# Soft MoE behind attention on one core: a group's shifts, its combine steps, the experts' loads and the borrowed parts in another order

## The chip, the cores and the metric

The kernel runs on one core of a Trainium2 chip. The metric is the device time of one execution in microseconds. It was run three times before the change; the median counts.

## The reference

Attention without softmax runs over 8 batches of 2496 tokens; its output, 19968 rows of 256, goes through a soft mixture of 8 experts with 4 slots each. Cut to what matters:

```python
scores = (z @ z.transpose(0, 2, 1)) / S        # z: 8 x 2496 x 64
x = u * (np.maximum(scores, 0.0) ** 2 @ v)     # u, v: 8 x 2496 x 256
x = x.reshape(B * S, D)
logits = x @ phi                               # 19968 x 32
d = np.exp(logits - logits.max(0)); d /= d.sum(0) + 1e-09
slot_input = d.T @ x                           # 32 slots
# each expert: h = np.maximum(slot_input[e] @ w1[e], 0.0); slot_out[e] = h @ w2[e]
c = np.exp(logits - logits.max(1, keepdims=True)); c /= c.sum(1, keepdims=True) + 1e-09
out = c @ slot_out
```

## The kernel before

**Half steps.** The attention is cut into half steps, 50 for each of batches 0 to 6 (numbers 0 to 349) and 60 for the last (350 to 409). A half step takes two tiles of 128 keys against a chunk of up to 512 queries; ten of them in a row (their place is `at`, 0 to 9) make a chunk of x. The main loop (line 1001) handles half step h: it calls `transfers(h)` (line 905, DMAs that come due), then `weights(last)` (experts' loads by the number of half steps that are left, `W_LOADS`, line 854, from 58 before the end on), then one item of the list `work` if `at` is at least 2 or 20 or fewer are left, and then TensorE's sums of half step h, with `prepare` (line 428) of half step h+3 in their midst, h+2 in the first ones.

**What `prepare(k)` does.** TensorE writes the scores of k (line 352) to `sc`, the only tile of the pool `sc_ps` (line 90). ScalarE reads it with a relu to `r` and squares `r`. The values are then split in two 16-bit parts: the high part `ph` is a cast by ScalarE or VectorE, the low part `pl` is VectorE's difference `r` minus `ph`; TensorE sums `ph` and `pl` times v into `acc`. Since the scores are symmetric, parts are reused: VectorE transposes `r` to `y` (a half step that turns) and SyncE stores it (`turned`), so that a later half step fetches its `r` and needs no scores (a turned half step; ScalarE only casts). A half step whose keys are its own queries takes half of its values so: one half step transposes to `yd` and lends them (`lent`, line 487), the next fetches them as `rd` (`borrow`, line 497) and does scores for the other half only (128x2x256 for the relu). `transfers` calls `borrow(k)` up to 5 half steps ahead of k (line 917).

**Two lists.** What `work` puts into `middle` is run on ScalarE between the relu and the square of the next `prepare` (for a turned half step ahead of its cast); what it puts into `behind` is run at the end of it, on VectorE.

**Groups.** The rows of x are taken in groups of 1024 (0 to 19), and `groups(q)` (line 626) makes the list of 15 items that `work` then hands out one per half step, so over two chunks, eight for each (`todo`, line 778, for groups 0 to 17). Its items: `logits` (products of x and phi, copied to `L` by VectorE); `ex` (the dispatch exponential `E`, into `middle`); four `blocks` and `e` (transposes of x and of E to `y`, behind); four `shifts` (each issues four DMAs of a quarter from `y` to `xt`, so that slots and tokens lie for the slot sums); `c0` (`combine`: transpose of `L` in place, its maximum `rm`, the difference, all on VectorE); `c1` (`combine_exp`: exponential of `L` on ScalarE, into `middle`); `c2` (`combine_sum`: sum, add, reciprocal and product); `c3` (the transpose to `cw`) together with an entry for the slot sums in `late`. The slot sums of group q (line 708) run on TensorE within `logits` of group q+1 and read `xt`.

**Order.** Each engine works in the order in which the program is written (`InOrder`). SyncE issues every DMA, in one queue. All engine calls go through one helper, so the trace gives line 74 for them and the tiles tell them apart.

Of the kernel before, what the change touches and what calls it, by code (L numbers as in the profile page):

```python
# [77 lines left out]
def attn_soft_moe_kernel(ctx, tc, uT, v, zz, phi, ww, outT):  # L78
# [37 lines left out]
    def take_blocks(b):  # L116


        for j in BLOCKS[b == B - 1]:
            zt[b, j] = blk.tile([P, 2, 512], F16, tag="blk", name=f"z_{b}_{j}")  # L120
        for i in range(2 * NP):
            vt_[b, i] = blk.tile([P, 2, 2, D], F16, tag="blk", name=f"v_{b}_{i}")
# [202 lines left out]
    pend, arriving, scratch, staged = {}, {}, {}, {}  # L325
# [5 lines left out]
    def run(todo):  # L331
        now, todo[:] = todo[:], []
        for f in now:
            f()

    def fetch(k):

        x = halves[k]
        j, o, n, _ = x.ch
        if n < PAD + PAD:  # L340
            r = wa.tile([P, 2, 4, P], F32, tag="r", name=f"r_{k}", bufs=4)
        else:
            r = turns_sb.tile([P, 4, 4, P], F32, tag="y", name=f"r_{k}")
        a0, na = o // P, r.shape[1]
        sp.dma_start(
            r.rearrange("p a j r -> p a (j r)"), scratch[x.b, x.p, j][:, a0 : a0 + na]
        )
        for i in range(2):
            w = halves[k + i].w
            arriving[k + i] = r[:, :, 2 * w : 2 * w + 2].rearrange("p a h r -> p h a r")  # L350
# [146 lines left out]
    def borrow(k):  # L497

        x = halves[k]
        r = turns_sb.tile([P, 4, 2, 2 * NS], F32, tag="rd", name=f"rd_{k}", bufs=1)  # L500
        sp.dma_start(r.rearrange("p a j r -> p a (j r)"), scratch.pop((x.b, x.p, x.p)))
        arriving[k] = r.rearrange("p a j r -> p j a r")
# [117 lines left out]
    def shift(src, a):  # L620


        for b in range(4):
            sp.dma_start(xt[32 * b : 32 * b + 32, a], src[32 * a : 32 * a + 32, b])

    def groups(q):
# [6 lines left out]
        def own(tag, *shape):  # L633
            if tag not in tiles:
                tiles[tag] = wk.tile([P, *shape], F32, tag=tag, name=f"{tag}_{q}", bufs=1)
            return tiles[tag]

        L, E, y = lambda: own("L", 2 * P), lambda: own("E", 2 * P), lambda: own("y", 4, NB)
# [36 lines left out]
        def turn_block(j, c):  # L675
            dve.transpose(
                y()[:, :, j * D : (j + 1) * D].rearrange("p b (t c f) -> p c t b f", t=4, c=2)[:, c],
                x[:, c, 512 * j : 512 * (j + 1)].rearrange("p (t b k) -> p t b k", t=4, b=4),
            )
# [50 lines left out]
        def turn_x_whole(i):  # L730
            j, t0 = i // 2, i % 2 * 2
            ps = ms_ps.tile([P, 2, 512], F32, tag="ms", name=f"xt_{q}_{i}")
            for k in range(2):
                turn_x(ps[:, k], x, 4 * j + t0 + k)
            for k in range(2):
                copy_x(act.copy, ps[:, k, 0:D], xt[:, t0 + k, j * D : (j + 1) * D])
# [34 lines left out]
        blocks = [lambda j=j, c=c: behind.append(lambda: turn_block(j, c)) for j in range(2) for c in range(2)]  # L771
        shifts = [lambda a=a: shift(y(), a) for a in range(4)]
        e, c0, c2, c3 = (lambda f=f: behind.append(f) for f in (turn_e, combine, combine_sum, combine_turn))
        ex, c1 = (lambda f=f: middle.append(f) for f in (exps, combine_exp))
        rest = lambda: None
        if q < NQG - 2:

            todo = [logits, ex, *blocks, e, shifts[0], c0, shifts[1], c1, shifts[2], c2, shifts[3]]
            todo.append(lambda: (c3(), late.append(slot_sums)))
        else:  # L780


            todo = [rest, rest, logits, ex, lambda: behind.append(adding.pop(0)), lambda: behind.append(add_counts)]
            todo += [c0, c1, c2, c3, turn_e_whole, *[lambda i=i: turn_x_whole(i) for i in range(4)]]
            todo.append(lambda: late.append(last_slot_sums))
# [36 lines left out]
    def load_w(i):  # L822
        t = w_raw[i]
        if isinstance(t, list):
            for k in range(2):
                sp.dma_start(t[k], ww[i][:, k * 512 : (k + 1) * 512])
        else:
            sp.dma_start(t, ww[i].rearrange("p (k n) -> p k n", k=2))
# [31 lines left out]
    def weights(left):  # L860

        if left in W_TAKES:
            W_TAKES[left]()
        for i in W_LOADS.get(left, ()):
            load_w(i)


    def load_u(b, ch):
        _, _, n, t0 = ch
        ut = wa.tile([P, 2, QC], F32, tag="ut", name=f"ut_{t0}", bufs=1)  # L870
        q0 = t0 - b * S
        sp.dma_start(
            ut[:, :, :n], uT[b, :, q0 : q0 + n].rearrange("(c p) q -> p c q", p=P)
        )
        ut_[t0] = ut
# [21 lines left out]
    landing, fetched = {}, set()  # L897
    accs = []

    def next_acc():  # L900

        accs.append(acc_ps.tile([P, 2, QC], F32, tag="acc", name=f"acc_{len(accs)}"))
        return accs[-1]

    def transfers(h):

        x = halves[h]
        if x.at == 2:
            load_u(x.b, x.ch)
        for k in range(h + 1, min(h + 9, len(halves))):  # L910
            y = halves[k]

            if y.turned and y.opens and k not in arriving and k not in fetched:
                if k - h <= 7 and (y.b, y.p, y.ch[0]) in scratch:
                    fetched.add(k)
                    fetch(k)
            if y.borrows and k - h <= 5 and k not in fetched and (y.b, y.p, y.p) in scratch:
                fetched.add(k)
                borrow(k)
        for f, b, i, at in splits.get(h + 2, ()):  # L920
            if (b, 0) not in vt_:
                take_blocks(b)
            for step, g in zip(at, f(b, i), strict=True):
                landing.setdefault(step, []).append(g)
        if h in later:
            landing.setdefault(h, []).append(later[h])
        while stores and stores[0][0] <= h + 1:
            stores.pop(0)[1]()

    def split_first_v():  # L930
        if v_splits:
            for f in v_splits.pop(0):
                f()
# [3 lines left out]
    def between_last(k):  # L937

        if k:
            if k == 1:  # L940
                xps.append(sc_ps.tile([P, 2, QC], F32, tag="sc", name="tr_first"))
                two = [raws.tile([P, 2, D], F32, tag="raw", name=f"xt_last_{i}", bufs=NRAW) for i in range(2)]
                xt_last.extend(t[:, i] for t in two for i in range(2))
            ps = xps[0][:, k - 1, 0:D]
            turn_x(ps, xg_[NQG - 1], k - 1)
            copy_x(act.copy, ps, xt_last[k - 1])
# [54 lines left out]
    for h, x in enumerate(halves):  # L1001
        if x.begins:
            chunk = h // (2 * NP)
            acc = accs[chunk] if chunk < len(accs) else next_acc()
        last = len(halves) - h
        transfers(h)
        weights(last)
        if work and (x.at > 1 or last <= 20):
            work.pop(0)()
        behind.extend(landing.pop(h, ()))  # L1010
        ahead = [k for k in range(h + 2 + (h > CATCH), h + 3 + (h >= CATCH)) if k < len(halves) and k >= 3]
        split_first_v()
        if not ahead and h < 1:
            run(middle)
            run(turning)
            run(behind)
            sums_halves(h, acc, 1, sums_halves(h, acc, 0, None))
        elif ahead and not halves[ahead[0]].turned:
            turn = sums_halves(h, acc, 0, None)
            prepare(ahead.pop(0))  # L1020
            sums_halves(h, acc, 1, turn)
        else:
            if ahead and not x.ends:
                prepare(ahead.pop(0))
            elif not ahead:
                run(middle)
                run(behind)
                between_last(3 - last)
            sums_whole(h, acc)
        if x.ends:  # L1030
            finish_chunk(x.b, x.ch, acc)
        for k in ahead:
            prepare(k)
        if h in FIRST_Z:
            z_splits.pop(FIRST_Z[h])()
        del pend[h]
# [300 lines left out]
```

## Time and profile before

| | us |
|---|---|
| runs | 1304.5, 1305.19, 1307.16 |
| median | 1305.19 |
| span of the profiled execution | 1303.9 |
| TensorE (PE) busy | 1259.8 |
| VectorE (DVE) busy | 1100.0 |
| ScalarE (ACT) busy | 933.8 |

The profiled execution has no time of its own beside the span; the median of the runs is 1.3 us above it. In the rows further down a line gives an engine, the operation, the tile that it writes and those that it reads; brackets give idle time of the engine ahead of the instruction and what ended it. A semaphore wait is put down to the event that came last by the profile. The granted clock is TensorE's, 1.00 being 2.4 GHz and 0.50 being 1.2 GHz.

### The profile page before, as it was taken

The page shows a single profiled execution, that of the slowest core. Times are in us where ns is not written, and L with a number is a line of the kernel's source. Part 1 is how long each engine was busy: PE and PEld are TensorE (multiplying, and loading weights), DVE is VectorE, ACT ScalarE, POOL GpSimd, SP SyncE. Part 2 cuts the span into 40 slices and gives each one's busy share as a digit, 9 for nine tenths or more (in the row PEclk, how much of TensorE's full clock was granted, in tenths as well). Part 3 has the DMA queues.
Part 4 walks back from the last instruction along what each step waited for, and adds up shares of the span by engine and source line. Part 5 has one row for each costly group of instructions (what it writes and reads, how often), then busy time and mean ns, then how long its engine had stood idle before and what let it go on. Part 6 is the DMA issues. An engine that isn't in the chain of part 4 may idle for free.

```text
span 1303.9 us, 27620 instructions
## 1 busy us (share of the span) xinstructions
PE 1259.8 (97%) x10961; PEld 609.2 (47%) x10961; DVE 1100.0 (84%) x1587; ACT 933.8 (72%) x1217; POOL 3.7 (0%) x22
## 2 busy tenths in 40 slices
PE   7999999999999999999999999999999999899984
PEld 3444454444544444444544444444544444345752
DVE  6888898789998899789998899789998799766663
ACT  6878697686857788586958688486977778554553
POOL 0000000000000000000000000000000000000000
PEclk7999999999999999999999999999999999999985
DMA  4868758793788757894788757886688858979769
GB/s 138 230 186 263 237 123 241 245 285 120 195 281 269 251 125 224 259 274 152 175 265 274 239 144 211 258 280 192 147 246 267 250 161 229 283 208 321 290 251 379
DMA packets 136402, 298.88 MB, mean 229 GB/s; under 512 B 17872, under 2 KB 38864, under 8 KB 124240
## 3 DMA queue, kind: packets, MB, share of 16 engines
q1 hardware_dynamic: 136272, 297.11, 74.4%
q8 instruction: 86, 1.41, 0.4%
q14 instruction: 44, 0.36, 0.1%
HBM read 162.04 MB, written 113.77 MB: 212 GB/s over the span
## 4 chain that ended last, share of the span: by engine, by line
PE 80%; ACT 7%; DMA 5%; DVE 3%; SPq 2%; issue 2%; ACTq 0%; DVEq 0%; POOLq 0%
PE acc L74 64%; PE sc L74 10%; ACT r L74 4%; PE lg L74 3%; SPq L74 2%; PE pf L74 2%; DMA w_own<-in_w 1%; DMA xt<-y 1%; DVE pl L74 1%; ACT ph L74 1%; ACT ot L74 1%; ACT v L74 1%; DVE y L74 1%; DMA rd<-lent 1%; DMA turned<-y 1%
## 5 line engine op out<-in xcount | busy, mean ns | idle before, releaser
L74 PE MATMUL acc<-ph,v 64*128 64x512 f16 (+5 forms) x5036 | 932.1, 370 | 3.1 <-DVE ph L74 2.0
L74 PEld LDWEIGHTS <-v 64*128 64x128 f16 (+1 forms) x7554 | 470.5, 95 | 527.9 <-issue 40.3
L74 PE MATMUL acc<-pl,v 64*128 64x512 f16 (+5 forms) x2518 | 603.1, 369 | 1.5 <-DVE pl L74 1.2
L74 DVE TENSOR_TENSOR pl<-r,ph 128x1024 f16<-128x1024 f32 (+1 forms) x410 | 466.5, 1146 | 109.6 <-ACT ph L74 98.1
L74 ACT CAST ph<-r 128x1024 f16<-128x1024 f32 (+1 forms) x286 | 288.6, 1018 | 134.3 <-DMA r<-turned 73.2
L74 ACT ACTIVATE r<-sc 128x1024 f32<-128x1024 f32 (+1 forms) x242 | 229.1, 947 | 126.2 <-PE sc L74 124.1
L74 ACT ACTIVATE r<-r 128x1024 f32<-128x1024 f32 (+1 forms) x241 | 237.4, 985 | 6.9
L74 DVE STREAM_TRANSPOSE y<-r 128x1024 f32<-128x1024 f32 x160 | 198.0, 1237 | 0.0
L74 PE MATMUL sc<-z,z 64*128 64x512 f16 x912 | 124.5, 377 | 2.7 <-ACT r L74 2.5
L74 PEld LDWEIGHTS <-z 64*128 64x128 f16 x1380 | 71.1, 94 | 76.5 <-issue 7.6
L74 DVE CAST ph<-r 128x1024 f16<-128x1024 f32 (+1 forms) x124 | 74.1, 598 | 12.9 <-ACT r L74 12.7
L74 DVE SCALAR_TENSOR_TENSOR xg<-acc,out_by,ut 128x1024 f32<-128x1024 f32 (+7 forms) x57 | 51.7, 930 | 10.1 <-PE acc L74 10.1
L74 DVE SCALAR_TENSOR_TENSOR v<-vr,v_by,v 128x512 f16<-128x512 f32 x80 | 57.9, 724 | 0.1
L74 ACT ACTIVATE v<-vr,v_by 128x512 f16<-128x512 f32 x80 | 57.0, 715 | 0.5 <-DVE v_by L74 0.5
L74 ACT ACTIVATE vq<-vr 128x512 bf16<-128x512 f32 x79 | 49.2, 623 | 9.8 <-DMA vr<-in_v 9.5
L74 PE MATMUL sc<-z 64*128 64x512 f16 (+1 forms) x468 | 50.6, 321 | 0.0
L74 DVE STREAM_TRANSPOSE y<-xg 128x512 f32<-128x512 f32 x72 | 49.4, 686 | 0.0
L74 DVE COPY ot<-pf 128x1024 f32<-128x1024 f32 (+1 forms) x20 | 24.0, 1198 | 20.7 <-PE pf L74 20.7
L74 ACT COPY ot<-pf 128x1024 f32<-128x1024 f32 (+1 forms) x20 | 19.8, 991 | 24.4 <-PE pf L74 21.5
L74 ACT CAST ph<-rd 128x512 f16<-128x512 f32 x36 | 21.8, 605 | 18.6 <-DMA rd<-lent 18.6
L74 DVE TENSOR_TENSOR pl<-rd,ph 128x512 f16<-128x512 f32 x36 | 24.0, 666 | 13.0 <-ACT ph L74 12.9
L74 PE MATMUL lg<-xt 64*32 64x256 f32 x576 | 23.7, 392 | 8.5 <-DMA w_raw<-in_w 5.0
(187 smaller groups left out, 540.2 us busy)
## 6 DMA issues: line engine op xcount, KB each, us to landing
turned<-y SPq DMA_DIRECT2D x320, 256.0 KB, 4.9
r<-turned SPq DMA_DIRECT2D x76, 1024.0 KB, 6.4
xt<-y SPq DMA_DIRECT2D x288, 72.0 KB, 3.6
vr<-in_v SPq DMA_DIRECT2D x80, 256.0 KB, 5.4
outT<-ot SPq DMA_DIRECT2D x18, 1024.0 KB, 7.0
ut<-in_uT SPq DMA_DIRECT2D x31, 512.0 KB, 6.2
lent<-yd SPq DMA_DIRECT2D x144, 64.0 KB, 2.9
rd<-lent SPq DMA_DIRECT2D x36, 256.0 KB, 4.3
```

The lines of the kernel that those rows point to most:

```text
L74: return lambda *a, **k: self.tc.keep_in_program_order(f(*a, **k))
```

## The change

In a group's list all four shifts now follow `e` (in which the transposed exponentials are put behind), and `c0`, `c1` and `c2` come after them in three half steps in a row; they had a shift between each two. An experts' load is issued behind the item of `work`, not ahead of it. A borrowed part may be fetched six half steps ahead, not five.

```diff
-            todo = [logits, ex, *blocks, e, shifts[0], c0, shifts[1], c1, shifts[2], c2, shifts[3]]
+            todo = [logits, ex, *blocks, e, *shifts, c0, c1, c2]
             todo.append(lambda: (c3(), late.append(slot_sums)))
...
-            if y.borrows and k - h <= 5 and k not in fetched and (y.b, y.p, y.p) in scratch:
+            if y.borrows and k - h <= 6 and k not in fetched and (y.b, y.p, y.p) in scratch:
...
         transfers(h)
-        weights(last)
         if work and (x.at > 1 or last <= 20):
             work.pop(0)()
+        weights(last)
```

In the rows of the order that follow, a name ends in the number of a half step or group and a running number of the program: `r_57_2355` is `r` of half step 57, `L_1_1885` is `L` of group 1.

ScalarE around half steps 57 to 60, before:

```order
L74 ACTIVATE L_1_1885<-L_1_1885 128x256
L74 ACTIVATE r_57_2355<-r_57_2355 128x1024
L74 CAST ph_57_2366<-r_57_2355 128x1024
L74 ACTIVATE r_58_2406<-sc_58_2407 128x1024
L74 ACTIVATE r_58_2406<-r_58_2406 128x1024
L74 CAST ph_58_2416<-r_58_2406 128x1024
L74 ACTIVATE r_59_2446<-sc_59_2447 128x2x256
L74 ACTIVATE r_59_2446<-r_59_2446 128x2x256
L74 CAST ph_59_2456<-rd_59_2340 128x8x64
L74 ACTIVATE r_60_2515<-sc_60_2516 128x1024
```

And after the change:

```order
L74 ACTIVATE r_58_2406<-sc_58_2407 128x1024
L74 ACTIVATE r_58_2406<-r_58_2406 128x1024
L74 CAST ph_58_2416<-r_58_2406 128x1024
L74 ACTIVATE r_59_2449<-sc_59_2450 128x2x256
L74 ACTIVATE L_1_1885<-L_1_1885 128x256
L74 ACTIVATE r_59_2449<-r_59_2449 128x2x256
L74 CAST ph_59_2460<-rd_59_2292 128x8x64
L74 ACTIVATE r_60_2511<-sc_60_2512 128x1024
L74 ACTIVATE r_60_2511<-r_60_2511 128x1024
```

The exponential of `L` of group 1 moved from between relu and square of half step 57 to between those of half step 59.

VectorE at the same place, before, with the three steps of `c0` on `L_1` behind the first transpose:

```order
L74 STREAM_TRANSPOSE y_55_2274<-r_55_2260 128x2x16x32
L74 STREAM_TRANSPOSE L_1_1885<-L_1_1885 128x256
L74 TENSOR_REDUCE rm_1_1800<-L_1_1885 128x8
L74 TENSOR_TENSOR L_1_1885<-L_1_1885,rm_1_1800 128x256
L74 CAST ph_56_2323<-r_56_2313 128x1024
L74 TENSOR_TENSOR pl_56_2324<-r_56_2313,ph_56_2323 128x1024
L74 STREAM_TRANSPOSE y_55_2274<-r_56_2313 128x2x16x32
L74 TENSOR_TENSOR pl_57_2367<-r_57_2355,ph_57_2366 128x1024
L74 STREAM_TRANSPOSE y_57_2370<-r_57_2355 128x2x16x32
```

And after the change:

```order
L74 TENSOR_TENSOR pl_58_2417<-r_58_2406,ph_58_2416 128x1024
L74 STREAM_TRANSPOSE y_57_2374<-r_58_2406 128x2x16x32
L74 STREAM_TRANSPOSE L_1_1885<-L_1_1885 128x256
L74 TENSOR_REDUCE rm_1_1800<-L_1_1885 128x8
L74 TENSOR_TENSOR L_1_1885<-L_1_1885,rm_1_1800 128x256
L74 TENSOR_TENSOR pl_59_2461<-rd_59_2292,ph_59_2460 128x8x64
L74 CAST ph_59_2460<-r_59_2449 128x8x64
L74 TENSOR_TENSOR pl_59_2461<-r_59_2449,ph_59_2460 128x8x64
```

`c0` moved from behind half step 56's first transposes to behind that of half step 58, directly ahead of the low part of 59.

VectorE around half step 130, where the four steps on `rm_4` and `L_4` are `c2` of group 4, before:

```order
L74 TENSOR_TENSOR pl_129_5221<-r_129_5210,ph_129_5220 128x8x64
L74 TENSOR_REDUCE rm_4_4547<-L_4_4678 128x8
L74 TENSOR_SCALAR rm_4_4547<-rm_4_4547 128x8
L74 RECIPROCAL rm_4_4547<-rm_4_4547 128x8
L74 TENSOR_TENSOR L_4_4678<-L_4_4678,rm_4_4547 128x256
L74 CAST ph_130_5276<-r_130_5266 128x1024
L74 TENSOR_TENSOR pl_130_5277<-r_130_5266,ph_130_5276 128x1024
L74 STREAM_TRANSPOSE yd_130_5280<-r_130_5266 128x2x8x32
L74 SCALAR_TENSOR_TENSOR z_3_0_4395<-zr_3_0_4410,z_by1_85,z_3_0_4395 128x512
L74 TENSOR_TENSOR pl_131_5302<-r_131_5089,ph_131_5301 128x1024
```

And after the change:

```order
L74 CAST ph_130_5272<-r_130_5262 128x1024
L74 TENSOR_TENSOR pl_130_5273<-r_130_5262,ph_130_5272 128x1024
L74 STREAM_TRANSPOSE yd_130_5276<-r_130_5262 128x2x8x32
L74 TENSOR_REDUCE rm_4_4547<-L_4_4678 128x8
L74 TENSOR_SCALAR rm_4_4547<-rm_4_4547 128x8
L74 RECIPROCAL rm_4_4547<-rm_4_4547 128x8
L74 TENSOR_TENSOR L_4_4678<-L_4_4678,rm_4_4547 128x256
L74 SCALAR_TENSOR_TENSOR z_3_0_4395<-zr_3_0_4410,z_by1_85,z_3_0_4395 128x512
L74 TENSOR_TENSOR pl_131_5302<-r_131_5090,ph_131_5301 128x1024
```

`c2` moved from ahead of half step 130's cast to between its transpose and the low part of 131.

SyncE's queue near half step 369, where `xt` is a shift of group 16, `w_own` and `w_raw` are experts' loads, `turned` is a store and `rd`, `r` are fetches, before:

```order
L74 DMA r_370_14447<-turned_7_0_1_14379 128x2048
L74 DMA w_own_0_13941<-in_w 128x1024
L74 DMA xt_99<-y_16_14128 32x576 x4
L74 DMA rd_369_14488<-lent_7_0_14269 128x512
L74 DMA turned_7_0_2_14532<-y_365_14430 32x4x512 x4
L74 DMA w_own_0_13942<-in_w 128x1024
L74 DMA xt_99<-y_16_14128 32x576 x4
L74 DMA r_373_14582<-turned_7_4_1_13931 128x2048
L74 DMA turned_7_0_3_14629<-y_367_14518 32x4x512 x4
L74 DMA w_raw_7_13943<-in_w 128x512
L74 DMA w_raw_7_13944<-in_w 128x512
L74 DMA xt_99<-y_16_14128 32x576 x4
```

And after the change:

```order
L74 DMA ut_17920_14401<-in_uT 128x2x512
L74 DMA xt_99<-y_16_14128 32x576 x4
L74 DMA rd_369_14448<-lent_7_0_14269 128x512
L74 DMA r_370_14450<-turned_7_0_1_14379 128x2048
L74 DMA xt_99<-y_16_14128 32x576 x4
L74 DMA w_own_0_13981<-in_w 128x1024
L74 DMA xt_99<-y_16_14128 32x576 x4
L74 DMA turned_7_0_2_14536<-y_365_14434 32x4x512 x4
L74 DMA w_own_0_13982<-in_w 128x1024
L74 DMA r_373_14585<-turned_7_4_1_13931 128x2048
L74 DMA turned_7_0_3_14629<-y_367_14522 32x4x512 x4
L74 DMA w_raw_7_13983<-in_w 128x512
```

The shifts of group 16 moved closer together and ahead of the loads of `w_raw`, and the fetch of `rd_369` moved ahead of that of `r_370`.

## Rows read from the trace of the kernel before

**Rows 1.** The busy time of each engine, with its share of the span and its count of instructions, from the page's first part.

```profile
PE 1259.8 (97%) x10961; PEld 609.2 (47%) x10961; DVE 1100.0 (84%) x1587; ACT 933.8 (72%) x1217; POOL 3.7 (0%) x22
```

**Rows 2.** TensorE's waits, grouped by what it was about to write and by what ended the wait: us in total, how many, the longest in us.

```profile
PE sc L74 <- ACT r L74: 3.6, 9, 1.1
PE lg L74 <- DMA xt<-y: 3.4, 5, 0.9
```

**Rows 3.** The timeline of TensorE: start in us, duration of the group of like instructions in us, what, how many; in brackets the idle time ahead and what ended it. Slot sums of an early group, those of group 16, and scores a little behind them.

```profile
476.92 1.07 PE L74 MATMUL lg<-xt 64*32 64x256 f32 x32
...
1141.77 2.20 PE L74 MATMUL lg<-xt 64*32 64x256 f32 x32 [5.05 <-DMA w_raw<-in_w]
...
1146.44 1.29 PE L74 MATMUL sc<-z,z 64*128 64x512 f16 x6
```

**Rows 4.** The timeline of SyncE's DMA queue ahead of that wait: start, duration of the issuing, what, how many.

```profile
1132.52 3.18 SPq L74 DMA_DIRECT2D w_raw<-in_w  x2
...
1135.74 2.42 SPq L74 DMA_DIRECT2D xt<-y  x4
```

**Rows 5.** Busy times by stretch. The columns are the stretch, its length, the busy time of PE, PEld, DVE, ACT and POOL with counts, TensorE's mean granted clock, the DMA engines' mean busy share, and GB/s.

```profile
1141.80:1144.00 2.20, 2.20 (x34) 1.17 (x36) 0.00 (x0) 0.00 (x0) 0.00 (x0) 0.50 0.77 142
1144.00:1146.00 2.00, 2.00 (x10) 0.63 (x12) 1.65 (x6) 0.00 (x0) 0.00 (x0) 0.50 0.94 316
1146.00:1148.00 2.00, 2.00 (x14) 0.79 (x12) 0.00 (x0) 0.22 (x1) 0.00 (x0) 0.65 1.04 299
1150.00:1160.00 10.00, 10.00 (x100) 4.51 (x98) 8.90 (x11) 9.64 (x13) 0.00 (x0) 1.00 0.25 62
1160.00:1200.00 40.00, 40.00 (x288) 18.93 (x284) 30.90 (x42) 20.40 (x27) 0.00 (x0) 1.00 0.97 290
```

**Rows 6.** The timeline of TensorE at the sums of the borrowed half steps 67 and 369.

```profile
225.96 0.60 PE L74 MATMUL acc<-ph,v 128*128 128x512 f16 x2 [1.00 <-DVE ph L74]
...
1126.71 0.60 PE L74 MATMUL acc<-ph,v 64*128 64x512 f16 x4 [0.96 <-DVE ph L74]
```

**Rows 7.** ScalarE's waits ahead of the combine exponential: us in total, how many, the longest.

```profile
ACT L L74 <- DVE L L74: 15.1, 11, 2.6
```

**Rows 8.** Timelines around half steps 57 to 61: ScalarE (the exponential and the square of half step 57, the square and cast of 58, the square and the cast of the borrowed part of 59, the relu of 60), VectorE (the first and the last step of `c0`, then the low part and the transpose of 58), and TensorE (the scores of 58 and of 61; then those of the same steps in half steps 308 and 311).

```profile
190.06 0.42 ACT L74 ACTIVATE L<-L 128x256 f32<-128x256 f32 x1 [1.06 <-DVE L L74]
190.38 1.04 ACT L74 ACTIVATE r<-r 128x1024 f32<-128x1024 f32 x1
...
193.45 1.06 ACT L74 ACTIVATE r<-r 128x1024 f32<-128x1024 f32 x1
194.54 1.05 ACT L74 CAST ph<-r 128x1024 f16<-128x1024 f32 x1
...
196.12 0.63 ACT L74 ACTIVATE r<-r 128x512 f32<-128x512 f32 x1
196.66 0.60 ACT L74 CAST ph<-rd 128x512 f16<-128x512 f32 x1
197.16 1.02 ACT L74 ACTIVATE r<-sc 128x1024 f32<-128x1024 f32 x1
...
188.71 0.40 DVE L74 STREAM_TRANSPOSE L<-L 128x256 f32<-128x256 f32 x1
...
189.60 0.42 DVE L74 TENSOR_TENSOR L<-L,rm 128x256 f32<-128x256 f32 x1
...
195.62 1.23 DVE L74 TENSOR_TENSOR pl<-r,ph 128x1024 f16<-128x1024 f32 x1 [0.25 <-ACT ph L74]
196.76 1.24 DVE L74 STREAM_TRANSPOSE y<-r 128x1024 f32<-128x1024 f32 x1
...
190.35 0.83 PE L74 MATMUL sc<-z,z 64*128 64x512 f16 x6
...
199.09 0.83 PE L74 MATMUL sc<-z,z 64*128 64x512 f16 x6
...
936.70 0.83 PE L74 MATMUL sc<-z,z 64*128 64x512 f16 x6
...
945.44 0.83 PE L74 MATMUL sc<-z,z 64*128 64x512 f16 x6
```

**Rows 9.** Timelines around half steps 38 and 39: ScalarE's cast of 38 and its square of 39, VectorE's last low part of 39, and TensorE's first use of the low part of 39.

```profile
136.11 1.04 ACT L74 CAST ph<-r 128x1024 f16<-128x1024 f32 x1
...
138.29 0.63 ACT L74 ACTIVATE r<-r 128x512 f32<-128x512 f32 x1
...
140.53 0.69 DVE L74 TENSOR_TENSOR pl<-r,ph 128x512 f16<-128x512 f32 x1
...
143.07 0.38 PE L74 MATMUL acc<-pl,v 128*128 128x512 f16 x1
```

**Rows 10.** Timelines around half steps 130 and 131: VectorE's low parts of the two, and TensorE's first use of each.

```profile
411.20 1.23 DVE L74 TENSOR_TENSOR pl<-r,ph 128x1024 f16<-128x1024 f32 x1
...
413.60 1.22 DVE L74 TENSOR_TENSOR pl<-r,ph 128x1024 f16<-128x1024 f32 x1
...
413.70 0.38 PE L74 MATMUL acc<-pl,v 128*128 128x512 f16 x1
...
416.29 0.38 PE L74 MATMUL acc<-pl,v 128*128 128x512 f16 x1
```

**Rows 11.** The timeline of TensorE at the first scores behind half step 149, where a batch begins.

```profile
473.99 0.82 PE L74 MATMUL sc<-z,z 64*128 64x512 f16 x6 [0.28 <-ACT r L74]
```

## The prediction

> **What bounds the kernel now.** I read four views in this order. First the busy times of the engines: TensorE is busy for nearly the whole span, VectorE and ScalarE for less [rows 1]. So the time is TensorE's work plus its gaps, and an edit counts by the gaps that it closes or opens there. Second, what TensorE waits for. The waits fall into few kinds: the transposed copy `xt` that the slot sums read (3.4 us over five places), the single score tile that ScalarE hasn't emptied yet (3.6 us over nine) [rows 2], one long wait of 5.05 us ahead of the slot sums of group 16 [rows 3], and two of about 1 us for the cast of a borrowed half step [rows 6]. Third, what ScalarE waits for: 15.1 us for VectorE's `L` [rows 7]. Those waits hardly reach TensorE today. The fourth view is the order of the steps around them, because the change moves exactly that exponential.
>
> **The change, part by part: what it removes.**
> *Shifts earlier.* The last of a group's four shifts is issued three half steps sooner than before. In the five short waits the piece that lands last is what TensorE waits for; three half steps are some 8.7 us (scores of 58 at 190.35 to those of 61 at 199.09, [rows 8]), far more than the longest wait of 0.9, so all 3.4 us go.
> *Group 16.* The 5.05 us stand under the name of an experts' load, but the slot sums read `xt`: SyncE issued two of these loads at 1132.52 and the last shift only behind them, at 1135.74 [rows 4], 1 us before the wait begins. Both edits pull this shift ahead of the loads. Behind the wait the granted clock was 0.50 for 2.20 us, 0.50 for 2.00 and 0.65 for 2.00 [rows 5], the lower of the two levels (1.2 GHz) or between them; at 1.00 the work of these stretches takes 0.50, 0.50 and 0.65 of the time, so 1.1 + 1.0 + 0.7 = 2.8 us are lost. The rows agree: the slot sums' 32 products took 2.20 us there and 1.07 elsewhere [rows 3]. Together 5.05 + 2.8 = 7.85 us.
> *Borrowing one half step sooner.* The fetched half of a borrowed score tile came too late twice, at half step 67 (1.00) and at 369 (0.96) [rows 6]. The first goes whole. At 369 the exponential of group 16 now stands ahead of the same cast on ScalarE and takes a part of it back: between 0 and 1.0 I take 0.6. Together 1.6.
> Removed: 3.4 + 7.85 + 1.6 = 12.9 us.
>
> **What it adds.** No instruction; but `c0` (transpose, maximum, difference of `L` on VectorE, put behind a half step) and `c1` (its exponential on ScalarE, put into the next half step between relu and square) now stand in adjacent half steps, where one half step lay between them. ScalarE works in order: behind the exponential are queued the square of this half step, the cast and the next relu, which empties the only score tile. VectorE does `c0` behind the transpose of the previous half step. What I add up is how late that chain is against TensorE's need.
>
> *Groups 1, 3, 8 and 13 (half steps 59, 109, 209, 309).* All from [rows 8]. The scores of 58 end at 190.35 + 0.83 = 191.18. The exponential that made ScalarE wait 1.06 in half step 57 is gone from there, so relu of 58 starts at once: relu 1.02, square 1.06 and cast 1.05 end at 194.4 with the small steps between them. On VectorE the low part and the transpose behind it take from 195.62 to 198.00, 2.4 us, so they end at 196.8; `c0` takes from 188.71 to 190.02, 1.3, and ends at 198.1. The exponential starts then; the square follows 0.32 behind its start (190.06 to 190.38) and takes 0.63, the cast of the borrowed part starts 0.54 behind the square, relu of 60 another 0.50 behind that (the rows' starts 196.12, 196.66, 197.16) and lasts 1.02: it ends at 198.1 + 0.32 + 0.54 + 0.50 + 1.02 = 200.5. TensorE wants this tile for the scores of 61 at 199.09. So it waits 1.4 us, four times: 5.6. The last of the four places has the same step from score to score (936.70 to 945.44, 8.74, as 190.35 to 199.09), so I cost them alike.
>
> A rule of the Trainium skill (page "Perfetto Trace Analysis", section "Matmuls") wants independent products to rotate through several banks of PSUM, so that emptying one overlaps filling the next. This kernel has one score tile, and the row of 3.6 us shows TensorE waiting for it, so trace and rule agree; if the scores did rotate, the 5.6 would be nothing and the sum below would be 2.1 us under the time before. No run shown here does that.
>
> *Groups 0, 2, 7 and 12 (39, 89, 189, 289).* From [rows 9]. The cast of 38 (136.11, 1.04) comes 0.3 sooner, without the exponential in half step 37, and ends at 136.85. Low part and transpose 2.4, `c0` 1.3: 140.6. The exponential, and 0.32 behind its start the square: 140.9. From the square to the end of the last low part were 138.29 to 141.22, 2.93, so that part is ready at 143.85. TensorE wants it at 143.07: 0.8 late, four times 3.2.
>
> *Groups 4, 9 and 14 (129, 229, 329).* The same chain, 0.8. The low part of 130 started at 411.20 and lasted 1.23; pushed back by 2.4 (`c0` 1.3, exponential 0.3, and 0.8 of the way round over ScalarE) it ends at 414.8, wanted at 413.70 + 0.8 (TensorE is late by that much already): 0.3 more. `c2` moves from ahead of half step 130 to between it and 131, 1.3 us on VectorE as `c0`: the low part of 131 (413.60, 1.22, ready 414.82) comes 2.3 + 1.3 later, at 418.4, and is wanted at 416.29 + 1.1 [rows 10]: 1.0 more. 2.1 a place, 6.3 in all; the most uncertain term, as small spans add up here over three half steps.
>
> *Groups 5, 10 and 15 (149, 249, 349).* A batch begins here, ScalarE also prepares v and z, and TensorE waits 0.28 for the tile already [rows 11]. By the same shift of ScalarE I work out 0.3 to 0.5 for the three: 1.3 in all. The shortest bound is 0, the longest the 1.4 of the first kind for each, 4.2; the place is nearer to 0.28, so 1.3.
>
> *Groups 6, 11 and 17* meet turned half steps, where the score tile is free and the exponential stands ahead of a cast with slack: 0. If that slack were gone, 0.8 each as in 39, 2.4.
>
> Added: 5.6 + 3.2 + 6.3 + 1.3 = 16.4 us; bounds 8 (each place half as late) and 21.7 (the two longest bounds above). *Moving the experts' loads* one item back adds no instruction, only their place behind three pieces of `xt`; nothing waits for them at the places shown, so 0.
>
> **Sum.** 16.4 - 12.9 = +3.5 us on the profiled span of 1303.9, 1307.4. The median of the runs, 1305.19, is 1.3 above that span, so 1308.7.
>
> **Rivals.**
> *A. The added stalls are half as long.* ScalarE reaches half step 59 sooner than I think, or VectorE does `c0` in a gap. 1305.2 - 12.9 + 8.2 = 1300.5. For it: the fifteen places are sums of short spans. Against: every step in them is in program order.
> *B. The other side: the waits go and nothing comes.* Place: ScalarE at the half steps behind `c0`. It decides at 1.4 us: if ScalarE has its relu of 60 done that much sooner than I have it, TensorE doesn't see the exponential, as it hardly saw the 15.1 us of such waits so far (3.6 at the score tile) [rows 2, 7]. Price: all 16.4 fall away, 1305.2 - 12.9 = 1292.3. Against it: those 15.1 us had a half step more of room, and four of the places are computed to come past the need by 1.4.
> The Trainium skill (the same page, section "Optimization Strategy") asks to find the gaps of the engine that bounds and to let what they wait for start sooner; that is what the edits do, and the rule by itself ends at B's time.
> *C. The end is bound by transfers.* From 1160 to 1200 the DMA engines are 0.97 busy [rows 5], so TensorE, 7.85 us sooner there, would only wait for fetched scores instead, and the group-16 gain is given back: 1308.7 + 7.85 = 1316.5. Against it: from 1150 to 1160 the share is 0.25, some 7 us of free transfer time that an earlier TensorE leaves in place, and TensorE was busy all 40 us that follow.
> *D. Only the first stall of each place is real*, and the knock-on ones at 130, 131 and the batch starts vanish: 5.6 + 3.2 + 3 x 0.8 = 11.2, 1303.5.
>
> **How the numbers follow.** Main case (1305.5 to 1312, from the bounds of its terms) 0.52; A 0.15; B 0.10; C 0.13; D 0.10. A measurement of this kernel tells about 0.2%, 2.6 us, from no change: below 1302.6 is faster, above 1307.8 slower. Faster holds B, most of A, no D: 0.21. Within 0.2%: D, the rest of A and the lower third of the main case, 0.31. Slower: two thirds of the main case and C, 0.48. The predicted time is the main case's, 1308.7. The range leaves B out and reaches over A and to C: 1298 to 1316. The main case alone has 1305.5 to 1312.
>
> **What would show it.** In the profile after: TensorE's waits for `xt` and the 5.05 us gone, the granted clock 1.00 around 1141; ScalarE's wait for `L` up from 15.1 to 35 or 40 us; TensorE's wait for the score tile up from 3.6 to some 10, with about 1.4 at each scores row behind half steps 59, 109, 209 and 309; new waits for low parts of about 0.8 to 1.0 near 143, 415 and 417. I am wrong if TensorE shows no new waits at these places (B), or if a wait for fetched scores shows up behind 1160 (C).

## The result and the profile after

| | before | after |
|---|---|---|
| median of the runs, us | 1305.34 (4 runs) | 1316.07 (4 runs, 1315.05 to 1317.46) |
| span of the profiled execution | 1303.9 | 1315.7 |
| TensorE busy | 1259.8 | 1259.1 |

The change made the kernel slower: the ratio is 1.0074, with a 95% interval of 1.0056 to 1.0092. TensorE is as busy as before, so the loss is in its gaps. These are its waits in the profile after (us in total, how many, the longest in us); they answer to [rows 2]:

```profile
PE sc L74 <- ACT r L74: 7.4, 10, 1.2
PE lg L74 <- DVE few L74: 6.2, 4, 1.6
PE acc L74 <- DVE pl L74: 5.9, 10, 0.9
PE acc L74 <- DVE ph L74: 3.6, 7, 0.7
PE acc L74 <- DVE v L74: 3.0, 4, 1.1
```

The waits for `xt` and for an experts' load are gone. In their place stand the score tile, the casts and low parts, the scaled v, and a new kind of 6.2 us: the logits (`lg`) wait for `few`, a small tile of VectorE's. ScalarE's wait that answers to [rows 7]:

```profile
ACT L L74 <- DVE L L74: 54.0, 19, 5.7
```

TensorE's instructions stand in the same order in both kernels, so its n-th matmul of one can be set beside the n-th of the other. The start after minus the start before, read along the span, shows where time went. The table has what each place adds; the half steps are those that the places of the prediction name:

| place | us |
|---|---|
| casts and low parts of half steps 39, 89, 189, 289, with the scores just ahead of them | +1.05, +0.90, +1.24, +1.52 = +4.7 |
| logits a little behind them (150, 299, 598, 897 us before) | +1.64, +1.77, +1.77, +1.76 = +6.9 |
| scores behind half steps 59, 109, 209, 309 | +1.41, +1.41, +1.41, +1.42 = +5.65 |
| half steps 129 to 131, 229 to 231, 329 to 331 | 3 x 2.23 = +6.7 |
| starts of batches behind 149, 249, 349 | +0.49, +0.95, +0.70 = +2.15 |
| half steps behind 390 (1209 to 1226 us after) | +3.5 |
| slot sums that waited for `xt`, six places | -7.4 |
| borrowed casts at 67 and 369 | -1.45 - 0.98 = -2.4 |
| group 16: the wait, and the clock behind it | -5.25 - 2.78 = -8.0 |

The sum is 29.6 - 17.8 = +11.8, as much as lies between the two spans.

The place that the prediction worked out in most detail, half steps 58 to 61, in the timelines after (columns as in [rows 8]): VectorE's transpose of 58 and `c0`, then ScalarE's exponential, cast and relu, then TensorE's scores.

```profile
198.27 1.24 DVE L74 STREAM_TRANSPOSE y<-r 128x1024 f32<-128x1024 f32 x1
199.43 0.40 DVE L74 STREAM_TRANSPOSE L<-L 128x256 f32<-128x256 f32 x1
...
200.78 0.42 ACT L74 ACTIVATE L<-L 128x256 f32<-128x256 f32 x1 [3.19 <-DVE L L74]
...
202.13 1.01 ACT L74 ACTIVATE r<-sc 128x1024 f32<-128x1024 f32 x1
...
203.20 0.82 PE L74 MATMUL sc<-z,z 64*128 64x512 f16 x6 [1.23 <-ACT r L74]
```

The chain is there step by step. ScalarE stands idle for 3.19 us in front of the exponential; the relu that empties the tile ends at 203.14, and the next scores start then.

The place that the prediction missed. A batch's largest values are found here: TensorE turns `few` into `mx`, a tile of the pool `ms_ps` that has one buffer, VectorE reads it (and writes `few` anew), and the logits take the same buffer. First VectorE before the change: the low part of the borrowed half of half step 39, the last step of `c2`, and the reading of `mx`. Then the same after the change, with the last step of `c0` ahead of it and the logits behind it:

```profile
139.49 0.67 DVE L74 TENSOR_TENSOR pl<-rd,ph 128x512 f16<-128x512 f32 x1
...
142.02 0.42 DVE L74 TENSOR_TENSOR L<-L,rm 128x256 f32<-128x256 f32 x1
...
149.83 0.28 DVE L74 TENSOR_REDUCE few<-mx 128x2 f32<-128x128 f32 x1
```

```profile
140.37 0.43 DVE L74 TENSOR_TENSOR L<-L,rm 128x256 f32<-128x256 f32 x1
142.31 0.69 DVE L74 TENSOR_TENSOR pl<-rd,ph 128x512 f16<-128x512 f32 x1 [1.51 <-ACT ph L74]
...
147.89 0.42 DVE L74 TENSOR_TENSOR L<-L,rm 128x256 f32<-128x256 f32 x1
...
152.69 0.28 DVE L74 TENSOR_REDUCE few<-mx 128x2 f32<-128x128 f32 x1
...
153.03 1.10 PE L74 MATMUL lg<-xg,phi_sb 64*32 64x256 f32 x32 [1.47 <-DVE few L74]
```

VectorE reads `mx` 2.86 us later. It is that late already at the low part, 2.82 us: `c0` (1.3 us) now stands just ahead of it, and behind `c0` VectorE waits 1.51 us for ScalarE's cast, which is queued behind the exponential. From the low part to the reading the profile shows no wait of VectorE, before or after, so nothing there takes the lateness up. `c2` adds nothing to it, as it stood ahead of this reading before the change too. TensorE wanted the buffer at 151.56.

Group 16 after, with the clock (columns as in [rows 3] and [rows 5]): no wait, 1.07 us for the slot sums, clock 1.00.

```profile
1153.59 1.07 PE L74 MATMUL lg<-xt 64*32 64x256 f32 x32
```

```profile
1152.00:1156.00 4.00, 4.00 (x82) 2.01 (x82) 0.18 (x1) 0.14 (x1) 0.00 (x0) 1.00 0.99 368
```

And the end, which was not in the sum either: SyncE's queue (columns as in [rows 4]) and two of TensorE's six waits behind it, with two of group 17's shifts in front of the fetches for half steps 392 and 394.

```profile
1198.73 3.51 SPq L74 DMA_DIRECT2D xt<-y  x4
1202.28 1.07 SPq L74 DMA_DIRECT2D w_blk<-in_w  x2
1203.40 2.42 SPq L74 DMA_DIRECT2D xt<-y  x4
1205.92 1.90 SPq L74 DMA_DIRECT2D r<-turned  x2
...
1210.85 0.38 PE L74 MATMUL acc<-ph,v 128*128 128x256 f16 x2 [0.55 <-ACT ph L74]
...
1217.11 0.28 PE L74 MATMUL acc<-pl,v 64*128 64x256 f16 x2 [0.72 <-DVE pl L74]
```

Before, the fetch stood ahead of the last two shifts:

```profile
1188.57 0.44 SPq L74 DMA_DIRECT2D r<-turned  x1
1189.22 3.08 SPq L74 DMA_DIRECT2D xt<-y  x4
```

TensorE is 9 us later here than before, and the fetch 17.

### The profile page after: what moved, and what is told of

Its sections match the earlier page's. It is cut to its first block, busy times and chain, and to the rows that moved or that the text cites. A ratio compares the mean times of both kernels' runs of the same rounds, so it can differ in the third digit from the quotient of the medians.

```text
span 1315.7 us, 27630 instructions
## 1 busy us (share of the span) xinstructions
PE 1259.1 (96%) x10961; PEld 608.6 (46%) x10961; DVE 1100.3 (84%) x1587; ACT 931.3 (71%) x1217; POOL 3.7 (0%) x22
## 3 DMA queue, kind: packets, MB, share of 16 engines
q8 instruction: 86, 1.41, 0.4%
## 4 chain that ended last, share of the span: by engine, by line
PE 58%; ACT 16%; DVE 11%; DMA 9%; issue 4%; SPq 1%; ACTq 0%; DVEq 0%; POOLq 0%
PE acc L74 45%; ACT r L74 8%; PE sc L74 8%; DMA r<-turned 6%; ACT ph L74 4%; DVE pl L74 4%; PE lg L74 3%; DVE y L74 2%; PE pf L74 2%; ACT vq L74 1%; DMA turned<-y 1%; ACT ot L74 1%; DMA vr<-in_v 1%; DVE rm L74 1%; DVE L L74 1%
## 5 line engine op out<-in xcount | busy, mean ns | idle before, releaser
L74 ACT ACTIVATE L<-L 128x256 f32<-128x256 f32 x19 | 7.9, 417 | 54.0 <-DVE L L74 54.0
L74 PE MATMUL lg<-xg,phi_sb 64*32 64x256 f32 x608 | 21.9, 382 | 6.9 <-DVE few L74 6.2
```

What stands on the lines that cost most here:

```text
L74: return lambda *a, **k: self.tc.keep_in_program_order(f(*a, **k))
```

## The experiments

The theory: the loss comes from the order of VectorE and ScalarE, with `c0`, `c1` and `c2` in adjacent half steps; the early shifts, the loads and the fetches bring what they were costed at. Rivals: SyncE's queue is crowded by early shifts; or the moved loads and fetches cost.

**The parts apart.** Run e1: loads and fetches moved, the list as before.

```diff
-            todo = [logits, ex, *blocks, e, *shifts, c0, c1, c2]
+            todo = [logits, ex, *blocks, e, shifts[0], c0, shifts[1], c1, shifts[2], c2, shifts[3]]
```

> The list of a group as before; only the experts' loads behind the group's item and the borrowed parts six half steps ahead. Theory (the combine steps in adjacent half steps are what costs): no new wait anywhere; the waits at 226 and 1127 go (1.4 and 1.0 us), and most of the 5.05 us and of the 2.8 us at half clock behind it, since the last shift of group 16 is issued ahead of two loads: about 1296 us. Rival (the loads or the fetches, moved in SyncE's queue, are what costs): slower than before, or no faster.

Measured 1306.88 us, ratio 0.9997 (0.9978 to 1.0016): no difference, 11 us worse than the theory wanted; the rival's forecast (no faster) came out. Its waits for `xt` are the largest new kind (its profiled execution, 1309.4, is one of the slower ones of its runs, which lie between 1300.3 and 1310.1):

```profile
PE lg L74 <- DMA xt<-y: 11.3, 8, 2.7
```

So one of the two edits seems to make `xt` land later when the shifts come late. Run e2: the list alone, with the other two edits undone.

```diff
-            if y.borrows and k - h <= 6 and k not in fetched and (y.b, y.p, y.p) in scratch:
+            if y.borrows and k - h <= 5 and k not in fetched and (y.b, y.p, y.p) in scratch:
...
         transfers(h)
+        weights(last)
         if work and (x.at > 1 or last <= 20):
             work.pop(0)()
-        weights(last)
```

> Only the new list of a group; loads ahead of the item and borrowed parts five half steps ahead, as before. Theory: all added waits of the changed kernel are there, and the two waits for the borrowed cast come back at most: 1316 to 1319 us. Rival (loads or fetches cost): close to 1300 us or under it.

Measured 1319.36 us, 1.0106 (1.0089 to 1.0123). That is 0.4 above the forecast; the list by itself gives the whole loss. Its profile has the added waits and none for `xt` or for an experts' load, so the list alone also does away with the wait at group 16. The borrowed cast at 369 waits 2.95 there. Run e6: the earlier fetch alone, on the kernel before.

```diff
-            if y.borrows and k - h <= 5 and k not in fetched and (y.b, y.p, y.p) in scratch:
+            if y.borrows and k - h <= 6 and k not in fetched and (y.b, y.p, y.p) in scratch:
```

> The kernel before, with the borrowed parts fetched six half steps ahead and nothing else. Theory (the earlier fetch stands in SyncE's queue ahead of stores and shifts, so xt lands later): the waits for xt grow from 3.4 to 9 us or more, some with half clock behind them, the waits at 226 and 1127 go: 1309 to 1316 us. Rival (a fetch of 256 KB six half steps ahead is free): 1302 to 1304 us.

Measured 1312.85 us beside 1306.05 of the kernel before, 1.0048 (1.0033 to 1.0063). It came out as the theory says. The waits at 226 and 369 are gone, but the waits for `xt` are 12.5 us over nine. SyncE's queue ahead of the slot sums of group 7 shows how the fetch `rd` holds the shifts up, first in the kernel before, then in this run:

```profile
691.49 2.77 SPq L74 DMA_DIRECT2D lent<-yd  x4
...
694.79 2.42 SPq L74 DMA_DIRECT2D xt<-y  x4
697.32 0.52 SPq L74 DMA_DIRECT2D rd<-lent  x1
```

```profile
694.94 2.61 SPq L74 DMA_DIRECT2D lent<-yd  x4
699.03 0.34 SPq L74 DMA_DIRECT2D rd<-lent  x1
...
699.88 2.43 SPq L74 DMA_DIRECT2D xt<-y  x4
```

Before, a shift was issued between the store `lent` and the fetch of the same values. Now the fetch comes first, the queue stands from 697.55 to 699.03, and the shift follows the start of the store by 4.9 us in place of 3.3. SyncE's waits for `lent` grew from 23.0 us over 20 to 33.3 over 30. That this is the whole cost was not tried.

In this run the clock falls behind a long wait for `xt`. The slot sums of group 4, and the stretch from there on (columns as in [rows 3] and [rows 5]):

```profile
420.86 2.39 PE L74 MATMUL lg<-xt 64*32 64x256 f32 x32 [1.72 <-DMA xt<-y]
```

```profile
420.80:424.50 3.70, 3.64 (x36) 1.43 (x37) 2.30 (x4) 0.07 (x1) 0.00 (x0) 0.56 0.93 281
```

Run e7: the loads alone, on the kernel before.

```diff
         transfers(h)
-        weights(last)
         if work and (x.at > 1 or last <= 20):
             work.pop(0)()
+        weights(last)
```

> The kernel before, with the experts' loads issued behind the group's item and nothing else. Theory: nothing changes up to about 1080 us; the wait of 5.05 us at group 16 falls to under 2 and the half clock behind it mostly goes: 1298 to 1302 us. Rival (the shift was late for another reason): within 1.5 us of the kernel before.

Measured 1305.00 us, 0.9988 (0.9975 to 1.0001): the expectation missed, and the rival's time came out. Its reason did so in part: the wait at group 16 fell to 2.48, not under 2, and the one for the borrowed cast at 369 grew to 2.03:

```profile
1129.46 0.60 PE L74 MATMUL acc<-ph,v 64*128 64x512 f16 x4 [2.03 <-DVE ph L74]
...
1143.57 2.63 PE L74 MATMUL lg<-xt 64*32 64x256 f32 x32 [2.48 <-DMA xt<-y]
```

This kernel's waits for `xt` came to 7.4 us against 3.4 before, some of them ahead of 1080 us where the two programs are the same. So these waits differ by some us from one execution to the next, and a single profile's sum of them is not exact.

**The list taken apart.** Run e3: early shifts, but the three combine steps where they were before (`rest` is an item that does nothing).

```diff
-            todo = [logits, ex, *blocks, e, *shifts, c0, c1, c2]
+            two = lambda: (shifts[1](), shifts[2]())
+            todo = [logits, ex, *blocks, e, shifts[0], c0, two, c1, shifts[3], c2, rest]
```

> As the changed kernel, but combine, its exponential and its sum stand where they stood before, in every other half step; the shifts still come early (the second and third share an item, the fourth is two half steps sooner than before). Theory (VectorE and ScalarE's order costs): the added waits at the score tile, for low parts and for the largest-value tile go, the gains for xt, loads and borrowed parts stay: 1288 to 1293 us. Rival (four shifts close together crowd SyncE's queue, so fetches and stores come late): as the changed kernel, 1312 us or more.

Measured 1303.60 us, 0.9974 (0.9963 to 0.9985). The four waits of 1.23 at the score tile and all waits for `few` are gone, and the run is 12.5 us under the changed kernel, so the rival falls as an account of the loss; but the run is 10 us above the range expected, and a crowded queue may have its part in that: waits for `xt` of 1.12 and 1.97 stand at 539 and 840, and behind 1140 and 1200 some of 0.65 to 0.78 for casts and low parts. Run e4 is the reverse, the combine steps in a row and the shifts late.

```diff
-            todo = [logits, ex, *blocks, e, *shifts, c0, c1, c2]
+            s2_c0, s3_c2 = lambda: (shifts[2](), c0()), lambda: (shifts[3](), c2())
+            todo = [logits, ex, *blocks, e, shifts[0], rest, shifts[1], rest, s2_c0, c1, s3_c2]
```

> Loads and borrowed parts as in the changed kernel; combine, its exponential and its sum in three half steps in a row as there, but the shifts at the places of the kernel before. Theory (the three steps in a row cost by VectorE's and ScalarE's order alone): the waits at the score tile at 202, 353, 657 and 961 (1.2 each), those of 1.5 for the largest-value tile and those for low parts are there as in the changed kernel; with late shifts on top, 1318 to 1332 us. Rival (the early shifts cost): within 5 us of the kernel that moved only loads and fetches, 1302 to 1312 us.

Measured 1326.00 us, 1.0148 (1.0125 to 1.0171): 19 us over run e1, in the range of the theory. Waits at the score tile 7.4, for `few` 6.2, as in the changed kernel. What separates the two possible reasons, a `c0` just put behind or a later half step without room, is run e5: `c0` one half step sooner, with the fourth shift in its old place, and `c1` and `c2` where the change has them.

```diff
-            todo = [logits, ex, *blocks, e, *shifts, c0, c1, c2]
+            todo = [logits, ex, *blocks, e, *shifts[:3], c0, shifts[3], c1, c2]
```

> As the changed kernel, but the combine step is one half step sooner and the fourth shift one later, so that a half step lies between combine and its exponential; exponential and sum stay where the changed kernel has them. Theory (the exponential waits for a combine that has just been put behind): the waits of 1.2 us at the score tile at 202, 353, 657 and 961 go, and most of the others: 1292 to 1300 us. Rival (it is the later half step that has no room for the exponential and the sum): within 4 us of the changed kernel, 1312 us or more.

Measured 1295.19 us, 0.9915 (0.9895 to 0.9936), faster than both kernels and 20.9 us under the changed one. VectorE's reading of `mx`, then ScalarE at half step 59 and TensorE's scores of 61:

```profile
149.81 0.28 DVE L74 TENSOR_REDUCE few<-mx 128x2 f32<-128x128 f32 x1
...
195.35 0.42 ACT L74 ACTIVATE L<-L 128x256 f32<-128x256 f32 x1 [0.48 <-DVE L L74]
...
197.12 1.02 ACT L74 ACTIVATE r<-sc 128x1024 f32<-128x1024 f32 x1 [0.33 <-PE sc L74]
...
199.06 0.83 PE L74 MATMUL sc<-z,z 64*128 64x512 f16 x6
```

The exponential waits 0.48 in place of 3.19, and it is the relu that waits for the scores, not the other way round. VectorE reads `mx` at 149.81, as early as before the change, and the waits for `few` are gone, with `c2` where the changed kernel has it: it was `c0`'s place that made the reading late. Run e8: the same with the fetch five half steps ahead.

```diff
-            if y.borrows and k - h <= 6 and k not in fetched and (y.b, y.p, y.p) in scratch:
+            if y.borrows and k - h <= 5 and k not in fetched and (y.b, y.p, y.p) in scratch:
```

> The list with combine one half step sooner (as in the run e5), loads behind the item, but borrowed parts five half steps ahead as before. Theory (the earlier fetch costs only where shifts come late, and here they come early): the waits at 226 and near 1120 come back, 2 to 3 us slower than e5, 1296 to 1299 us. Rival (the earlier fetch crowds the queue here too): faster than e5, 1290 to 1294 us.

Measured 1297.55 us, 0.9936 (0.9915 to 0.9958), within the range expected. But the wait at 226 did not come back; the one at half step 369 did, and longer:

```profile
1124.65 1.03 PE L74 MATMUL acc<-ph,v 64*128 64x512 f16 x4 [4.21 <-DVE ph L74]
```

The two intervals overlap, so the 2.4 us between the medians are in the direction expected but not settled.

**The terms alone.** The list of run e5, and the changed kernel's list in four groups only, in run e10 in 0, 2, 7 and 12, in run e11 in 1, 3, 8 and 13.

```diff
+            todo = [logits, ex, *blocks, e, *shifts[:3], c0, shifts[3], c1, c2]
+            if q in (0, 2, 7, 12):
+                todo = [logits, ex, *blocks, e, *shifts, c0, c1, c2]
```

> The list with combine one half step sooner (run e5), except that groups 0, 2, 7 and 12 have the changed kernel's list. Theory (each of these places costs by itself 1.1 us for the casts and low parts and 1.7 us where the logits wait for the largest-value tile): 4 x 2.8 = 11 us over e5, 1305 to 1307 us. Rival (the long waits at the logits come from lateness carried over from other groups): under 1300 us.

```diff
-            if q in (0, 2, 7, 12):
+            if q in (1, 3, 8, 13):
```

> As run e5, except that groups 1, 3, 8 and 13 have the changed kernel's list. Theory: the four waits of 1.23 us at the score tile and nothing else, 4 x 1.4 = 5.6 us over e5, 1299 to 1302 us. Rival (a wait of ScalarE at these places is taken up by TensorE's slack): as e5, 1294 to 1296 us.

Beside them, as their base, run e12 is e5 without an edit.

> Run e5 once more, beside the three others on the same chip, as their base: 1294 to 1296 us.

The base gave 1294.38 us, 0.9906 (0.9886 to 0.9926). Groups 0, 2, 7 and 12: 1304.81 us, 0.9990 (0.9976 to 1.0003), 10.4 over the base against 11 expected; the four waits for `few` are the same 6.2 us as in the changed kernel. Groups 1, 3, 8 and 13: 1299.48 us, 0.9952 (0.9934 to 0.9969), 5.1 over it against 5.6 expected. Set beside the profile of run e12 as above, the four places of e10 add 2.5, 2.7, 2.7 and 2.7 us and those of e11 1.41 each, as much as in the changed kernel (where 189 and 289 add 3.0 and 3.3). So both kinds stand by themselves. (The profiled execution of e11, the slowest of its runs, has besides a wait of 2.35 us at the slot sums at 543.)

**The end.** Run e9: the changed kernel, with group 17 alone on the list of before.

```diff
+            if q == NQG - 3:
+                todo = [logits, ex, *blocks, e, shifts[0], c0, shifts[1], c1, shifts[2], c2, shifts[3]]
```

> As the changed kernel, but group 17 alone keeps the list of before, so two of its four shifts no longer stand in SyncE's queue ahead of the fetch for half step 392. Theory (the six waits between 1210 and 1226 come from that fetch being issued behind two more shifts): they go, 2 to 3.5 us faster than the changed kernel, 1312 to 1314 us. Rival (the transfers of the end are full anyway): the fetch lands as late, 1316 us.

Measured 1317.23 us, 1.0089 (1.0062 to 1.0116), no faster than the changed kernel. The six waits are gone, as the theory says, so the fetch behind two more shifts did cause them; a wait for `xt` stands there in their place:

```profile
1211.81 1.09 PE L74 MATMUL lg<-xt 64*32 64x256 f32 x30 [0.53 <-DMA xt<-y]
```

In the profiles this place is 2.3 us shorter than in the changed kernel. The span, 1314.8, is only 0.9 shorter: waits at 548, 776 and 891, where the two programs are the same, add 2.2 us, and others differ too. So a gain of this size can't be told from one execution's differences. In the profile of run e12 the same half steps cost 3.0 us against the kernel before, so this loss doesn't come from the place of `c0`.

## Why the prediction came out as it did

The sign and the reason held: `c1` right behind `c0` costs TensorE more than the waits that the other edits remove. The size did not: +10.7 us in the medians (+11.8 in the spans) against +3.5. That 1316.07 lies at the upper end of the range, 1316, is luck: the range reached so far for rival C's 1316.5, and C's mechanism is not what happened. The main case's own range doesn't follow from its terms either: the bounds of 8 and 21.7 us give 1300.3 to 1314.0, not 1305.5 to 1312. By the steps of the prediction:

- *Groups 1, 3, 8, 13:* 5.6 forecast, 5.65 in the trace, 5.1 by itself in a run. Rival B, which lets the exponential vanish in TensorE's slack, falls with this; so does A, half of every stall.
- *Groups 4, 9, 14:* 6.3 forecast, 6.7 found. Rival D, which leaves the knock-on stalls out, falls: the 0.88 at half step 131 is one of them.
- *Groups 0, 2, 7, 12:* 3.2 forecast, 4.7 found at the casts and low parts, and 6.9 that the sum lacked. **This is the step that failed.** It followed VectorE's lateness (2.6 us by its own numbers, 143.85 against 141.22) to the next low part that TensorE needs and stopped there. The same lateness, 2.86 us, delayed VectorE's reading of `mx`, whose single buffer the logits want. Run e10, with these four groups alone, shows 10.4 us for both.
- *Starts of batches:* 1.3 forecast, 2.15 found, but at other tiles: TensorE waits for the scaled v and for `xg`, not for the scores.
- *Groups 6, 11 and 17* at nothing: so in their chains of exponentials. But *moving the shifts* had no price at all in SyncE's queue, and at the end it cost 3.5 us behind 1209. The sign that the prediction named for rival C, a wait for fetched scores behind 1160, did show, but not for C's reason: TensorE is not sooner there but 9 us later, and run e9 shows that the fetch's place behind two more shifts makes the waits. That the 3.5 us can be had back is not shown.
- *Group 16:* 7.85 forecast, 8.0 found. Right.
- *Waits for `xt`:* 3.4 forecast, 7.4 found. The view of waits counts only idle time ahead of a group of matmuls. Where the pieces land one after the other, the products wait within the group. It shows in the group's duration, as in group 4's before, which should have been held against the 1.07 us of [rows 3]:

```profile
419.70 1.61 PE L74 MATMUL lg<-xt 64*32 64x256 f32 x32
```

- *Borrowing sooner:* 1.6 forecast, 2.4 found. That it costs nothing elsewhere was wrong by itself: on the kernel before, in run e6, it costs 6.8 us, with the fetch in the queue ahead of a shift. With early shifts this doesn't show.
- *The signs:* ScalarE's wait for `L` rose to 54.0 us, not to 35 or 40, and the waits at the score tile to 7.4, not 10; the 1.4 us at each of the four scores rows, the new waits for low parts and the full clock at group 16 came as forecast.

Misses of 6.9 + 3.5 + 1.5 + 0.85 + 0.45 on the one side and 4.0 + 0.8 + 0.15 on the other make the 8.3 us between 3.5 and 11.8.

What stays open: why run e3 is 8.4 us slower than e5, though the last shift stands at the same place in both. The profiled executions differ by 3.9 only (e3's is its fastest run); there e3 loses 1.6 and 1.8 at the slot sums at 539 and 840, 1.9 at the scores from 730 on and 2.0 at the casts at 1141, and gains elsewhere. Why `xt` lands later there was not tried. Nor were the groups 4, 9 and 14 run by themselves.

## What to carry to other kernels

When a step on an engine that works in order becomes later, follow its lateness until it is used up, past the first engine that needs it: to every buffer whose release sits behind it, among them single buffers that unrelated steps share. Leave a step's worth of room between a producer and its consumer on another engine; here one half step (run e5, which also moves the fourth shift) was worth 21 us over 18 groups. A transfer that is pulled ahead in a queue can hold up those behind it, as the fetch in run e6 did; in these runs its price showed only where the shifts came late.

## What the runs showed of the hardware

The clock also fell behind a shorter wait than the one of 5.05 us. Behind 1.72 us at the slot sums of group 4, in run e6, the granted clock was 0.56 over 3.70 us, between the two levels and near the lower one of 0.50, so by these numbers the wait cost nearly twice its length (an estimate: 1.72 + 0.44 x 3.70 = 3.3 us). Behind 1.6 us at the logits of the changed kernel it stayed at 1.00 (columns as in [rows 5]):

```profile
607.70:611.40 3.70, 3.65 (x74) 2.10 (x75) 3.56 (x8) 1.67 (x2) 0.00 (x0) 1.00 0.96 318
```

What tells these two cases apart was not tried.
